# A gated-recurrence kernel with routed experts: chunk pieces in another order, and expert tiles from chunk 11 on

## The chip, the core and the metric

The kernel runs on one core of a Trainium2 chip. The metric is the time of one launch on the device, in microseconds (us). The engines are TensorE (PE: matmuls and transposes; its weight loads are PEld), VectorE (DVE), ScalarE (ACT), GpSimd (POOL) and SyncE (SP); each runs its own instructions in order and waits on semaphores. Sixteen DMA engines serve the loads and stores that SP, ACT and POOL issue.

## The reference

A gated linear recurrence over 4 batches, 8 heads, 768 steps and head dimension 48 gives rows of width 8 * 48 = 384. A router then picks two of eight experts for each of the 3072 rows, and the output is the weighted sum of the two experts' results.

```
for t in range(S):                                   # S = 768
    state = alpha[:, :, t, :, None] * state + k_t (outer) v_t
    y[:, :, t] = einsum('bhd,bhde->bhe', q[:, :, t], state)
x = y.transpose(0, 2, 1, 3).reshape(3072, 384)
noisy = x @ w_gate + log1p(exp(x @ w_noise)) * noise  # (3072, 8)
top2 = the two largest of each row; top2_w = softmax over them
for e in range(8):                                    # F = 1024
    for k in range(2):
        mask = top2[:, k] == e
        out[mask] += top2_w[mask, k, None] * (relu(x[mask] @ w1[e]) @ w2[e])
```

## The kernel before, in words

**Chunks.** The 3072 rows are 24 chunks of 128 steps (six to a batch). For chunk n, SP loads alpha, k, q and v. `prepare` (L252) turns alpha, k and q with TensorE transposes into a PSUM pool `tp` of two banks. ScalarE copies alpha into `a_all` (L257), runs a Relu over the same bank for a range test (L258), and copies k (L261). VectorE makes the running products `P_all` (scan, L264), q times them (L268), a reciprocal, and the reverse scan `over` (L273); GpSimd multiplies k by it (L275). `scores` (L281) has the k-q matmuls into two banks, the masked copies into `MT` (L291), and the transposes of k into `k_end` (L295, L297). `state` (L299) updates the state by a matmul (L309); `output` (L316) makes y (L189, L193) and copies it to `yT`; `turn_y` (L321) turns it and stores 128 rows of x (L203 to L206). `route` (L325) makes the logits (L211); after each third chunk it also runs `choose` (the two experts and their weights, VectorE and ScalarE, with table loads on ScalarE). `give` (L331) then ranks the rows (`rank`, L545; read by `picked`, L547), writes table entries by indirect DMA (L136), and plans tiles (`plan_tiles`: `total`, L579, and some 25 small VectorE operations up to L629). The PSUM pool `y` is a single bank: `s`, `lg`, `y`, `rank`, `total` and `count` share it.

**Tiles.** Three chunks are a unit, numbered from 0 to 7. After a unit is given, more full tiles of 128 rows of one expert are known. GIVEN says how many tiles stand ready after each unit: 0, 5, 11, 17, 23, 29, 35, and the rest; 51 tiles always run. Tiles 5 to 10, say, are those of unit 2, and unit 0 has none. A tile: its table rows (`load_tab`, L649), its w1 (1.5 MB, L657), a gather of its x rows (L675), a transpose `x_ps` and a VectorE copy `xt` (L684, L686), layer 1 in two halves (`h_ps`, L695, Relu L697), a gather of what the other expert has left of the rows (`prev` from `half_rows`, L714), layer 2 in two halves (`o_ps`, L707), the scaling (L724), a scatter into `half_rows` (L725), the sum (L731) and a scatter into the output (L732). `xt` has a single buffer, `prev` and w1 have two. All w2 (12.6 MB) is held on the chip, an expert's 1.5 MB per iteration over the first eight (L183).

**The order** is written by hand (L816 to L846): iteration n has a list of chunk pieces and a list of tile steps (four a tile), taken in turn, one of each. Tiles of unit u are beside iterations 3u+5 to 3u+7, two to an iteration at most, so the first is in iteration 8; unit 7's follow in one last iteration. In the iteration ahead of a unit's first tile, its tables and w1 are loaded, x is gathered, and, as the last piece, `turn_x` of that tile is run. The side buffer `half_rows` is zeroed at the start, by three DMAs of 1.5 MB from ScalarE's queue (L149 to L153).

Of the kernel before, what the change touches and what calls it, by code (L numbers as in the profile page):

```python
# [18 lines left out]
def kernel(  # L19
# [32 lines left out]
    C = 128  # L52
# [109 lines left out]
    def load_chunk(n, ins, vp):  # L162
        for x, src in (("a", alpha), ("k", k), ("q", q)):
            nc.sync.dma_start(out=ins[x][n % NIN][:, :, 0:D], in_=rows(src, n))
        vt = vp.tile([C, H, D], F32, name="vt")
        nc.sync.dma_start(out=vt, in_=rows(v, n))
        return vt
# [32 lines left out]
    def put_x(n, yT, on):  # L200
# [5 lines left out]
        nc.scalar.dma_start(out=x_rows[ds(n * C, C), :], in_=y_sb.rearrange("p j i d -> p (j i d)"))  # L206
# [8 lines left out]
    def fast_gla(on):  # L215
# [26 lines left out]
        def load(n):  # L242
            if n < NT:
                chunks[n] = {"v": load_chunk(n, ins, on["three"])}
# [7 lines left out]
        def prepare(n):  # L252
            if n >= NT:
# [4 lines left out]
            nc.scalar.activation(a_t, a_t, AF.Relu, bias=less_1, accum_out=above[:, n:n + 1])  # L258
            k_t = transposed(ins["k"][n % NIN])
            c["k"] = two.tile([C, NP, C], F32, name="k_P")  # L260
            nc.scalar.copy(c["k"], k_t)  # L261
            P_all = one.tile([C, NP * CB + 1], F32, name="P_all")
            P = P_all[:, 0:NP * CB].rearrange("p (j t) -> p j t", t=CB)
            nc.vector.tensor_tensor_scan(P_all[:, 0:NP * CB], a_all[:, 0:NP * CB],  # L264
                                         least.rearrange("p j t -> p (j t)"), 0.0, op0=ALU.mult, op1=ALU.max)
# [3 lines left out]


            over = one.tile([C, NP, CB], F32, name="over")
            nc.vector.reciprocal(out=P_all[:, CB::CB], in_=P_all[:, C::CB])
            nc.vector.tensor_tensor_scan(over.rearrange("p j t -> p (j t)")[:, :0:-1], a_all[:, :1:-1],  # L273
                                         P_all[:, :1:-1], 0.0, op0=ALU.mult, op1=ALU.max)
            nc.gpsimd.tensor_tensor(c["k"], c["k"], over[:, :, 1:CB], op=ALU.mult)  # L275
# [5 lines left out]
        def scores(n):  # L281
# [3 lines left out]
            sc = [on["sc"].tile([C, NP, C], F32, tag=f"sc{i}", name=f"sc{i}") for i in range(2)]  # L285
            for j in range(NP):
                for i in range(2):
                    r = ds(DP * i, D)
                    nc.tensor.matmul(sc[i][:, j, :], c["k"][r, j, :], c["q"][r, j, :], start=True, stop=True)  # L289
            for i in range(2):  # L290
                nc.vector.copy_predicated(MTs[n % 2][:, i], mask_upto, sc[i])  # L291
            if n % NCH != NCH - 1:
# [58 lines left out]
        return load, prepare, scores, state, output, turn_y, route, give, out_of_range  # L351


    def general_gla(es):
# [49 lines left out]
        def gla_prepare(n):  # L404
            vt = load_chunk(n, ins, vp)
# [226 lines left out]
    def experts(on):  # L632
# [80 lines left out]
        def get_half(i):  # L713
            get = nc.gpsimd.indirect_dma_start(out=prev[i % 2], out_offset=None, in_=half_rows,  # L714
                                               in_offset=bass.IndirectOffsetOnAxis(ap=wheres[i][:, 2:3], axis=0),
                                               bounds_check=N - 1, oob_is_err=False)
# [4 lines left out]
        def combine(i):  # L721
# [3 lines left out]
            put = nc.gpsimd.indirect_dma_start(out=half_rows,  # L725
# [15 lines left out]
    def tile_steps(i, do, units):  # L741
# [18 lines left out]
        def fourth():  # L760
            layer2(i, 1)
            combine(i)
# [137 lines left out]
```

## Time and profile before

| | us |
|---|---|
| median of 3 timed runs | 876.01 (875.53 to 878.22) |
| the profiled execution | 869.22 |
| its span, first to last instruction | 867.5 |
| TensorE busy in it | 773.0 |
| VectorE, ScalarE, GpSimd busy | 274.7, 198.4, 332.7 |
| mean granted TensorE clock | 0.951 of full |

A row of a timeline has start, duration, engine, line, operation, what is written and read, a count, and in brackets the engine's idle time ahead of it and what ended it. A row of the list of waits has the waiting and the awaited line, the us in total, how often, and the longest.

### The profile page before, as it was taken

The numbers are of one execution on the slowest core, as the hardware profiler recorded it, in microseconds if no ns is written. First come the engines' busy times: TensorE is split into PE (matmuls) and PEld (weight loads), VectorE is DVE, ScalarE is ACT, GpSimd is POOL, SyncE is SP. The second block draws the span as 40 slices with busy tenths as digits, with TensorE's granted clock in tenths as the row PEclk, the third lists the DMA queues.
The fourth block names the chain that finished last, engine by engine and source line by source line (L and its number), as shares of the span: only waits on it lengthen the run. The fifth ranks groups of instructions, "written<-read, shape, count | busy, mean of one in ns | idle before, by whom it ended". The sixth has DMA issues, their size and how long they took to land. (4 is left out here: it accounts for less than half of the span.)

```text
span 867.5 us, 14532 instructions
## 1 busy us (share of the span) xinstructions
PE 773.0 (89%) x5241; PEld 633.8 (73%) x5241; DVE 274.7 (32%) x969; ACT 198.4 (23%) x382; POOL 332.7 (38%) x436
## 2 busy tenths in 40 slices
PE   4878659997899999999998999999998999999992
PEld 3767548776687777877777877877876888888871
DVE  7455543234233531352324322431132111111110
ACT  2242402232123221321222222311121111111110
POOL 4224242326233732454334533353335333343331
PEclk9996859999799999999998999999999899999996
DMA  9997939443856277536673555426454345555530
GB/s 141 334 259 179 257 114 298 140 108 102 227 142 169 91 221 205 156 95 189 201 214 119 144 188 144 159 61 249 140 188 142 135 167 175 189 194 195 199 115 14
DMA packets 158532, 146.59 MB, mean 169 GB/s; under 512 B 119968, under 2 KB 132982, under 8 KB 158064
## 3 DMA queue, kind: packets, MB, share of 16 engines
q1 hardware_dynamic: 135904, 111.79, 44.6%
q0 software_dynamic: 14592, 23.75, 9.0%
q10 hardware_dynamic: 7952, 9.97, 3.5%
q8 instruction: 47, 0.77, 0.4%
q14 instruction: 37, 0.30, 0.1%
HBM read 131.95 MB, written 30.00 MB: 187 GB/s over the span
## 5 line engine op out<-in xcount | busy, mean ns | idle before, releaser
L695 PE MATMUL h_ps<-xt,w 128*128 128x128 f32 x2448 | 296.3, 281 | 8.6 <-DMA w<-in_moe_w_dram 4.7
L695 PEld LDWEIGHTS h_ps<-xt,w 128*128 128x128 f32 x2448 | 289.5, 197 | 17.1 <-DVE xt L686 5.7
L707 PE MATMUL o_ps<-w,h 128*128 x816 | 275.8, 487 | 0.0
L707 PEld LDWEIGHTS o_ps<-w,h 128*128 128x128 f32 x816 | 149.4, 190 | 89.3
L725 POOL DMA_INDIRECT half_rows<-o,where x51 | 58.4, 1146 | 264.7 <-ACT o L724 258.3
L697 ACT ACTIVATE h<-h_ps 128x512 f32<-128x512 f32 x102 | 60.8, 596 | 270.8 <-PE h_ps L695 270.8
L731 DVE TENSOR_TENSOR prev<-prev,o 128x384 f32<-128x384 f32 x51 | 28.5, 559 | 285.6 <-ACT o L724 153.0
L724 ACT ACTIVATE o<-o_ps,tab 128x384 f32<-128x384 f32 x51 | 29.7, 582 | 209.1 <-PE o_ps L707 207.0
L275 POOL TENSOR_TENSOR k_P<-k_P,over 128x512 f32<-128x512 f32 x24 | 28.4, 1183 | 111.1 <-DVE over L273 111.1
L675 POOL DMA_INDIRECT x_in<-x_rows,where x51 | 53.3, 1044 | 44.6 <-issue 20.4
L686 DVE COPY xt<-x_ps 128x384 f32<-128x384 f32 x51 | 28.3, 555 | 123.9 <-PE x_ps L684 123.9
L732 POOL DMA_INDIRECT out_dram<-prev,where x51 | 51.2, 1004 | 29.0 <-DVE prev L731 11.0
L714 POOL DMA_INDIRECT prev<-half_rows,where x51 | 53.0, 1039 | 21.0 <-issue 17.7
L136 POOL DMA_INDIRECT table<-entry,place_u x48 | 50.0, 1042 | 14.5 <-issue 12.2
L264 DVE TENSOR_TENSOR_SCAN P_all<-a_all,least 128x516 f32<-128x516 f32 x24 | 29.6, 1233 | 70.1 <-ACT a_all L257 68.3
L291 DVE COPY_PREDICATED MT<-upto,sc 128x512 f32<-128x512 uint32 x48 | 31.9, 719 | 17.8 <-PE sc L289 17.8
L684 PE MATMUL x_ps<-ident,x_in 128*128 128x128 f32 x153 | 27.1, 288 | 9.8 <-DMA x_in<-x_rows,where 9.8
L249 PE MATMUL tp<-ident,q_in 128*128 128x128 f32 x96 | 18.4, 322 | 18.1 <-ACT tp L258 17.4
L289 PEld LDWEIGHTS sc<-q_P,k_P 48*128 48x128 f32 x384 | 26.6, 210 | 8.1 <-issue 7.6
L289 PE MATMUL sc<-q_P,k_P 48*128 48x128 f32 x384 | 31.6, 310 | 0.0
L189 PE MATMUL y<-q_P,S 128*128 128x128 f32 x192 | 28.6, 297 | 2.8 <-ACT lgs L212 2.8
L273 DVE TENSOR_TENSOR_SCAN over<-a_all,P_all 128x515 f32<-128x515 f32 x24 | 29.6, 1235 | 0.8
(142 smaller groups left out, 649.8 us busy)
## 6 DMA issues: line engine op xcount, KB each, us to landing
w<-in_moe_w_dram SPq DMA_DIRECT2D x59, 1536.0 KB
a_in<-in_alpha_dram SPq DMA_DIRECT2D x24, 192.0 KB
k_in<-in_k_dram SPq DMA_DIRECT2D x24, 192.0 KB
q_in<-in_q_dram SPq DMA_DIRECT2D x24, 192.0 KB
vt<-in_v_dram SPq DMA_DIRECT2D x24, 192.0 KB
half_rows<-zeros ACTq DMA_DIRECT2D x3, 1536.0 KB
x_rows<-y_sb ACTq DMA_DIRECT2D x24, 192.0 KB
tab<-table SPq DMA_DIRECT2D x51, 2.0 KB
```

The source lines that it names most:

```text
L136: put = nc.gpsimd.indirect_dma_start(out=table, out_offset=bass.IndirectOffsetOnAxis(ap=place, axis=0), in_=entry, in_offset=None, bounds_ ...
L264: nc.vector.tensor_tensor_scan(P_all[:, 0:NP * CB], a_all[:, 0:NP * CB], least.rearrange("p j t -> p (j t)"), 0.0, op0=ALU.mult, op1=ALU.max)
L289: nc.tensor.matmul(sc[i][:, j, :], c["k"][r, j, :], c["q"][r, j, :], start=True, stop=True)
L291: nc.vector.copy_predicated(MTs[n % 2][:, i], mask_upto, sc[i])
L675: nc.gpsimd.indirect_dma_start(out=x_in[i % NB], out_offset=None, in_=x_rows[0:units * UT, :], in_offset=bass.IndirectOffsetOnAxis(ap=wher ...
L695: nc.tensor.matmul(h_ps[:, fo, :], w1[:, a, ds((part * FO // 2 + fo) * C, C)], xt[:, a, :], start=a == 0, stop=a == KO - 1)
L697: nc.scalar.activation(os_[i]["h"][part], h_ps, AF.Relu)
L707: nc.tensor.matmul(o["ps"], o["h"][part][:, f, :], w2[:, ds(o["e"], 1), fo, :].rearrange("p o d -> p (o d)"), start=fo == 0, stop=fo == FO ...
L714: get = nc.gpsimd.indirect_dma_start(out=prev[i % 2], out_offset=None, in_=half_rows, in_offset=bass.IndirectOffsetOnAxis(ap=wheres[i][:, ...
L724: nc.scalar.activation(o, o_ps, AF.Copy, scale=tab[:, 1:2])
L725: put = nc.gpsimd.indirect_dma_start(out=half_rows, out_offset=bass.IndirectOffsetOnAxis(ap=where[:, 1:2], axis=0), in_=o, in_offset=None, ...
L732: put = nc.gpsimd.indirect_dma_start(out=out, out_offset=bass.IndirectOffsetOnAxis(ap=where[:, 2:3], axis=0), in_=prev[i % 2], in_offset=N ...
```

## The change

The pieces of a chunk are cut finer and stand in another order: `prepare` becomes `alphas`, `keys` and `queries`; `scores` becomes `scores`, `masked` and `turn_k`; `load_chunk` leaves v to `load_v`, which comes behind `output`. `state` comes first in the iteration. `give` runs for chunk n-2 instead of n-1. The list of pieces is spread evenly over the tile steps. Tiles of unit u are beside iterations 3u+8 to 3u+10 (LAG = 8), so the first is in iteration 11. w2 is loaded in quarters of an expert, three an iteration over eleven iterations. `half_rows` is no longer zeroed; each chunk's rows are stored into it as well as into x. The router's loads and the table's clearing move behind iterations 0 and 1. Gathers from and scatters into `half_rows` name only the rows of units up to the tile's own.

```diff
-    def clear_half(on):
-        zeros = on.tile([C, KO * F], F32, tag="w1", name="zeros")
-        nc.vector.memset(zeros, 0.0)
-        for part in half_rows.rearrange("(i p r) d -> i p (r d)", p=C, r=KO * F // DM):
-            nc.scalar.dma_start(out=part, in_=zeros)
...
+    W2_PARTS = 4
-    def load_w2(e):
-        nc.sync.dma_start(out=w2[:, e], in_=moe_w2[e].rearrange("(a p) d -> p a d", p=C))
+    def load_w2(part):
+        e, f = divmod(part, W2_PARTS)
+        fs = ds(f * FO // W2_PARTS, FO // W2_PARTS)
+        nc.sync.dma_start(out=w2[:, e, fs], in_=moe_w2[e].rearrange("(a p) d -> p a d", p=C)[:, fs, :])
...
-        nc.scalar.dma_start(out=x_rows[ds(n * C, C), :], in_=y_sb.rearrange("p j i d -> p (j i d)"))
+        for dst in (x_rows, half_rows):
+            nc.scalar.dma_start(out=dst[ds(n * C, C), :], in_=y_sb.rearrange("p j i d -> p (j i d)"))
...
+        def keys(n):
...
             k_t = transposed(ins["k"][n % NIN])
             c["k"] = two.tile([C, NP, C], F32, name="k_P")
             nc.scalar.copy(c["k"], k_t)
+            nc.gpsimd.tensor_tensor(c["k"], c["k"], c.pop("over")[:, :, 1:CB], op=ALU.mult)
+        def queries(n):
...
             q_t = transposed(ins["q"][n % NIN])
             c["q"] = on["three"].tile([C, NP, C], F32, name="q_P")
             nc.vector.tensor_mul(c["q"], q_t, P[:, :, 1:C + 1])
...
-            get = nc.gpsimd.indirect_dma_start(out=prev[i % 2], out_offset=None, in_=half_rows,
+            get = nc.gpsimd.indirect_dma_start(out=prev[i % 2], out_offset=None, in_=half_rows[0:units * UT, :],
...
+        LAG = 8
-            u, part = divmod(n - UC - 2, UC)
+            u, part = divmod(n - LAG, UC)
-            if n >= UC + 2 and u < NU - 1 and GIVEN[u] > starts[u]:
+            if 0 <= u < NU - 1 and GIVEN[u] > starts[u]:
...
-                chunk = [lambda: prepare(n + 2), lambda: state(n), lambda: turn_y(n - 1), lambda: scores(n + 1),
-                         lambda: route(n - 1), lambda: output(n), lambda: load(n + 3), lambda: give(n - 1)]
-                if n < E:
-                    chunk.append(lambda: load_w2(n))
+                chunk = [lambda: (load(n + 3), state(n)), lambda: alphas(n + 2), lambda: keys(n + 2),
+                         lambda: scores(n + 1), lambda: (queries(n + 2), masked(n + 1)), lambda: route(n - 1),
+                         lambda: turn_k(n + 1), lambda: (output(n), load_v(n + 3)), lambda: turn_y(n - 1),
+                         lambda: give(n - 2)]
+                if n == 0:
+                    chunk.append(load_router)
+                if n == 1:
+                    chunk.append(lambda: clear_table(on["two"]))
+                chunk.append(lambda: [load_w2(i) for i in range(3 * n, min(3 * n + 3, E * W2_PARTS))])
                 if n == NT + 1:
                     chunk.append(out_of_range)
...
-                    chunk.insert(4, lambda: (load_w1(lo), [gather_x(i, u + 1) for i in some[:2]]))
+                    chunk.insert(6, lambda: (load_w1(lo), [gather_x(i, u + 1) for i in some[:2]]))
                     chunk.append(lambda: turn_x(lo))
-                for j in range(max(len(work), len(chunk))):
-                    if j < len(work):
-                        work[j]()
-                    if j < len(chunk):
-                        chunk[j]()
+                done = 0
+                for j in range(len(work)):
+                    work[j]()
+                    upto_j = len(chunk) * (j + 1) // len(work)
+                    for piece in chunk[done:upto_j]:
+                        piece()
+                    done = upto_j
+                for piece in chunk[done:]:
+                    piece()
```

On TensorE, a chunk's transposes beside a tile before (`h_ps` is layer 1, `tp` the transposes, `s` the state matmul):

```order
L695 MATMUL h_ps<-xt,w_1368 128x128 x12
L249 MATMUL tp<-ident,a_in_149 128x128 x4
L249 MATMUL tp<-ident,k_in_151 128x128 x4
L249 MATMUL tp<-ident,q_in_153 128x128 x4
L695 MATMUL h_ps<-xt,w_1368 128x128 x12
```

The same engine and place now, in an iteration with one tile (`sc` are the scores):

```order
L720 MATMUL h_ps<-xt,w_1985 128x128 x12
L332 MATMUL s_2140<-vt,k_end 128x96 x4
L255 MATMUL tp<-ident,a_in_149 128x128 x4
L720 MATMUL h_ps<-xt,w_1985 128x128 x12
L255 MATMUL tp<-ident,k_in_151 128x128 x4
L306 MATMUL sc_2201<-q_P,k_P 128x128
L306 MATMUL sc_2202<-q_P,k_P 128x128
...
L255 MATMUL tp<-ident,q_in_153 128x128 x4
```

The three groups of transposes stood together; layer 1 and the scores now stand between them.

On VectorE, the copy `xt` of a unit's first tile before, at the end of iteration 13 (`prev` is the sum of the two halves, `other` the next gather's test):

```order
L291 COPY_PREDICATED MT_169<-upto,sc_2769 128x512
L291 COPY_PREDICATED MT_169<-upto,sc_2770 128x512
L731 TENSOR_TENSOR prev_180<-prev_180,o 128x384
L686 COPY xt<-x_ps 128x384
L666 SCALAR_TENSOR_TENSOR other,before_it<-expert_idv,tab,given 128x8
```

The same copy now, at the end of iteration 16 (the rows up to `given` are the end of the plan that `give` makes):

```order
L651 TENSOR_REDUCE first<-row 128x6
L652 TENSOR_SCALAR plan<-first 128x6
L653 TENSOR_SCALAR plan<-of 128x6
L654 TENSOR_SCALAR given<-given 128x54
L756 TENSOR_TENSOR prev_180<-prev_180,o 128x384
L711 COPY xt<-x_ps 128x384
L691 SCALAR_TENSOR_TENSOR other,before_it<-expert_idv,tab,given 128x8
```

The plan, which was one iteration ahead of the copy, now stands directly in front of it.

On SyncE, the loads of one iteration of the alone stage before (`w_110` is w2):

```order
L166 DMA vt<-in_v_dram 128x8x48
L183 DMA w_110<-in_moe_w_dram 128x8x384
L164 DMA a_in_149<-in_alpha_dram 128x8x48
L164 DMA k_in_151<-in_k_dram 128x8x48
L164 DMA q_in_153<-in_q_dram 128x8x48
```

And now:

```order
L162 DMA vt<-in_v_dram 128x8x48
L182 DMA w_110<-in_moe_w_dram 128x2x384 x3
L158 DMA a_in_148<-in_alpha_dram 128x8x48
L158 DMA k_in_150<-in_k_dram 128x8x48
L158 DMA q_in_152<-in_q_dram 128x8x48
```

The order of the loads is the same; three quarters of an expert's w2 stand where one whole stood.

## Rows read from the trace of the kernel before

**Rows 1.** The page: busy us by engine, and TensorE's clock in 40 slices.
```profile
PE 773.0 (89%) x5241; PEld 633.8 (73%) x5241; DVE 274.7 (32%) x969; ACT 198.4 (23%) x382; POOL 332.7 (38%) x436
...
PEclk9996859999799999999998999999999899999996
```
**Rows 2.** Windows of the alone stage: busy us by engine, clock, DMA share, GB/s.
```profile
core 0: us, PE busy (x) PEld busy (x) DVE busy (x) ACT busy (x) POOL busy (x), PEclk, DMA share, GB/s
...
31.00:62.00 31.00, 25.79 (x238) 22.50 (x237) 15.84 (x24) 12.42 (x27) 7.29 (x14) 1.00 1.01 270
62.00:82.00 20.00, 16.23 (x99) 14.26 (x98) 9.08 (x35) 5.68 (x12) 8.91 (x14) 0.58 0.72 159
```
**Rows 3.** Waits: who waited for whom, us in total, times, longest.
```profile
PE tp L249 <- ACT tp L258: 17.4, 19, 1.3
...
PE total L579 <- DVE picked L547: 9.4, 7, 3.6
```
**Rows 4.** Timeline of TensorE in the alone stage, and the first h.
```profile
24.43 1.11 PE L249 MATMUL tp<-ident,k_in 128*128 128x128 f32 x4 [8.01 <-ACT k_end L297]
...
31.22 1.92 PE L189 MATMUL y<-q_P,S 128*128 128x128 f32 x8
...
61.10 1.13 PE L189 MATMUL y<-q_P,S 128*128 128x128 f32 x8 [0.35 <-ACT lgs L212]
...
66.14 0.59 PE L545 MATMUL rank<-chosen,before 128*128 128x24 f32 x2 [2.91 <-DVE past L535]
...
77.25 2.05 PE L189 MATMUL y<-q_P,S 128*128 128x128 f32 x8 [0.35 <-ACT lgs L212]
...
130.24 4.42 PE L695 MATMUL h_ps<-xt,w 128*128 128x128 f32 x24 [4.71 <-DMA w<-in_moe_w_dram]
```
**Rows 5.** DMA queues from 31 to 62 us: packets, MB, share of 16 engines.
```profile
q1 hardware_dynamic: 13543, 6.67, 85.6%
q10 hardware_dynamic: 405, 1.63, 14.5%
```
**Rows 6.** Timeline of TensorE beside tiles, and of two tiles alone.
```profile
161.96 2.84 PE L695 MATMUL h_ps<-xt,w 128*128 128x128 f32 x24
...
166.70 0.66 PE L249 MATMUL tp<-ident,q_in 128*128 128x128 f32 x4 [1.03 <-ACT tp L258]
...
171.07 2.75 PE L707 MATMUL o_ps<-w,h 128*128 x8
...
192.15 0.30 PE L545 MATMUL rank<-chosen,before 128*128 128x24 f32 x2
...
829.22 5.52 PE L695 MATMUL h_ps<-xt,w 128*128 128x128 f32 x48
...
840.06 5.52 PE L695 MATMUL h_ps<-xt,w 128*128 128x128 f32 x48
```
**Rows 7.** Timeline of TensorE at starts of units and at two late waits.
```profile
219.41 0.90 PE L684 MATMUL x_ps<-ident,x_in 128*128 128x128 f32 x3 [6.30 <-DMA x_in<-x_rows,where]
...
315.54 2.94 PE L695 MATMUL h_ps<-xt,w 128*128 128x128 f32 x24 [0.65 <-DVE xt L686]
...
472.17 0.60 PE L579 MATMUL total<-seen,ones 128*128 128x8 f32 x2 [3.56 <-DVE picked L547]
472.62 5.47 PE L695 MATMUL h_ps<-xt,w 128*128 128x128 f32 x24
...
673.21 0.59 PE L346 MATMUL count<-out_of,ones 128*128 128x2 f32 x2 [4.25 <-DVE out_of L344]
```
**Rows 8.** Timelines of VectorE (a plan's ends, a gather's offsets) and SyncE's queue.
```profile
283.99 0.20 DVE L547 TENSOR_TENSOR picked<-picked,rank 128x48 f32<-128x48 f32 x1
...
289.35 0.18 DVE L629 TENSOR_SCALAR given<-given 128x54 f32<-128x54 f32 x1
...
118.78 3.40 SPq L649 DMA_DIRECT2D tab<-table  x4
...
121.87 0.16 DVE L673 SCALAR_TENSOR_TENSOR where<-skip,tab 128x3 uint32<-128x3 f32 x1
```

More of the change, by code (lines that the diff above doesn't have):

```diff
@@ L243, in load, with load_v @@
             if n < NT:
-                chunks[n] = {"v": load_chunk(n, ins, on["three"])}
+                chunks[n] = {}
+                load_chunk(n, ins)
+        def load_v(n):
+            if n < NT:
+                chunks[n]["v"] = load_values(n, on["three"])
         def transposed(src):
@@ L250, in transposed, with alphas @@
             return tp
-        def prepare(n):
+        def alphas(n):
             if n >= NT:
@@ L261, in prepare @@
             nc.scalar.copy(c["k"], k_t)
[L262 to L265, printed above, removed]
+            nc.gpsimd.tensor_tensor(c["k"], c["k"], c.pop("over")[:, :, 1:CB], op=ALU.mult)
+        def queries(n):
+            if n >= NT:
+                return
+            c = chunks[n]
+            P = c.pop("P")
             q_t = transposed(ins["q"][n % NIN])
@@ L284, in scores @@
             c = chunks[n]
-            sc = [on["sc"].tile([C, NP, C], F32, tag=f"sc{i}", name=f"sc{i}") for i in range(2)]
+            c["sc"] = [on["sc"].tile([C, NP, C], F32, tag=f"sc{i}", name=f"sc{i}") for i in range(2)]
             for j in range(NP):
@@ L288, in scores, with masked, turn_k @@
                     r = ds(DP * i, D)
[L289 to L292, printed above, removed]
+                    nc.tensor.matmul(c["sc"][i][:, j, :], c["k"][r, j, :], c["q"][r, j, :], start=True, stop=True)
+        def masked(n):
+            if n < NT:
+                for i, sc in enumerate(chunks[n].pop("sc")):
+                    nc.vector.copy_predicated(MTs[n % 2][:, i], mask_upto, sc)
+        def turn_k(n):
+            if n < NT and n % NCH != NCH - 1:
+                c = chunks[n]
                 tp = on["tp"].tile([C, NP, C], F32, tag="tp", name="tp")
@@ L349, in out_of_range @@
             nc.vector.tensor_copy(out=again_i, in_=again)
-        return load, prepare, scores, state, output, turn_y, route, give, out_of_range
+        return (load, load_v, alphas, keys, queries, scores, masked, turn_k, state, output, turn_y, route, give,
+                out_of_range)
     def general_gla(es):
@@ L719, in get_half, with combine @@
             from_half.append(get.ins)
-        def combine(i):
+        def combine(i, units):
             o_ps, tab, where = os_.pop(i)["ps"], tabs.pop(i), wheres.pop(i)
@@ L756, in third @@
                 turn_x(i + 1)
-            get_half(i)
+            get_half(i, units[0])
             layer2(i, 0)
@@ L761, in fourth @@
             layer2(i, 1)
-            combine(i)
+            combine(i, units[0])
         return [first, second, third, fourth]
@@ L775 @@
         on = pools(es, "")
-        load, prepare, scores, state, output, turn_y, route, give, out_of_range = fast_gla(on)
+        (load, load_v, alphas, keys, queries, scores, masked, turn_k, state, output, turn_y, route, give,
+         out_of_range) = fast_gla(on)
         do = experts(on)
```

46 lines of the change are left out of this document (28 added, 18 removed).

## The prediction

> **What bounds the kernel now.** First the busy times: TensorE works 773.0 of 867.5 us, every other engine under 40% [rows 1]. So the time is TensorE's work, its idle time, and the time it runs at 1.2 instead of 2.4 GHz; the row of clocks shows the low level in slices near the start and in few later ones [rows 1]. Then TensorE's own timeline, by stage. Ahead of the first expert tile (its h at 130.24) chunks run alone; from there on tiles and chunks alternate.
>
> In the alone stage two things set the pace. The sixteen DMA engines are full, a share of 1.01 from 31 to 62 us [rows 2], and there three chunks take 61.10 − 31.22 = 29.9 us, 10.0 each [rows 4]. And where TensorE paused, its clock fell: the chunk with the wait of 2.91 us for `past` (rank at 66.14) took 77.25 − 61.10 = 16.2 us [rows 4], at a mean clock of 0.58 [rows 2].
>
> Beside the tiles, the list of waits [rows 3]: q's transposes wait for the Relu that frees one of the two `tp` banks, 19 times, 17.4 us; 14 of these stand beside tiles, with 14.3 us (166.70 is one [rows 6]). `total` waits for `picked`, 9.4 us, 9.1 of it beside tiles. The rest are starts of units, where `x_in`, `xt` or `count` is late [rows 7].
>
> The sum is made against the profiled execution, 869.22 us with a span of 867.5. The median of the timed runs is 876.01, 6.8 us more; I carry that difference over unchanged.
>
> **Chunks 8 to 10 leave the tiles: −22.4 us there.** The iteration from 161.96 to 192.15 is 30.19 us for two tiles and a chunk. A tile by itself takes 840.06 − 829.22 = 10.84 [rows 6]. So a chunk costs 30.19 − 21.68 − 1.03 (its q wait) = 7.48, three of them 22.4.
>
> **The q waits: −14.3 us.** Alphas, keys and queries now stand apart, with the scores or a step of a tile between them, so the Relu is done before q's transposes want the bank. Late next is the bank that x's transposes share with a and k; between them stands a step of layer 2, 2.75 us [rows 6], and a wait of 1.03 shows how little was missing with k's transposes alone between. Bounds 0 to −14.3; I take the whole.
>
> **`give` an iteration later: −9.6 us at `total`, +9.9 us at the starts of units.** Of the five gives beside tiles, four now stand ahead of the last step of layer 2, not behind the last `combine`, so `picked` no longer queues behind `prev` on VectorE. `total` then waits only for rank's own reader, some 0.4 us four times and 0.6 once, 2.2 in all. Before it was 9.1, and after the longest wait, 3.56, layer 1 took 5.47 us [rows 7] where the same row of 161.96 has 2.84 [rows 6]: about 2.7 us of low clock, 11.8 in all.
>
> But `turn_x` of a unit's first tile now comes behind the plan of the unit after it. VectorE copies `xt` only when that plan is done, 283.99 to 289.53, 5.5 us [rows 8], and layer 1 waits for `xt`. Unit 2: by my estimate the plan starts 1.2 us after the last matmul of layer 2 (o and `prev` come first), `xt` ends 7.4 after it, TensorE has 2.2 of work: 5.2 idle. Units 3 to 5: layer 2's second half covers 2.7 of it; from rank to `xt` are 7.2 us, TensorE's work 4.1: 3.1 idle. Unit 6 has `count` there, behind the longer last plan and `prev`: 4.5, and 0.65 for `xt`. Unit 7: 0.65. After idle times of 3.56 and 4.25 the clock fell (472.17, 673.21 [rows 7]), 2.7 us by the sum above; I charge that to units 2 and 6 and half of it to units 3 to 5. Sum: 7.9 + 3 × 4.45 + 7.85 + 0.65 = 29.8. Before: 6.30 + 0.65 + 2.7 at unit 2, 0.65 at four units, 4.25 + 0.65 + 2.7 at unit 7 [rows 7] = 19.9. So +9.9; bounds −4 (chain hidden, clock kept) to +19 (5.2 idle and the clock lost at each).
>
> **The alone stage: tile 0 starts at 137, not 130.24: +6.8 us.** The start: ScalarE no longer issues the clearing ahead of `k_end`, so the 8.01 us ahead of the k transposes at 24.43 go [rows 4], and y(0) starts near 23, not 31.22. The router's loads, now behind y(0) on ScalarE, take about 2 of that back. The pace: the first queue, with the loads of chunks and of w2, took 85.6% of 31 us for 13543 packets and 6.67 MB [rows 5]. An old iteration has 4 × 1024 packets of a chunk and 1024 of w2, 5120, hence 10.0 us. A quarter of w2 less is 256 packets or 0.39 MB: 0.5 us by packets, 1.8 by bytes, I take 1.1. The second copy of y is 0.2 MB on the other queue, which took 14.5% for 1.63 MB: 0.5 us [rows 5]. That makes 9.4; TensorE's own waits behind `choose` and `rank`, in six of the ten iterations, I leave in as 0.6: 10.0 an iteration (9.4 to 10.6), the old pace.
>
> Then y(1) starts at 35, y(9) at 35 + 8 × 10.0 = 115. Two us of y and 9 of v, w2 and a, k, q later the `tab` loads are issued, at 126 to 127. From there it is 3.25 us until the second tab's `where` is done (118.78 to 122.03 [rows 8]), then the plan, 5.5, and `xt`, 0.6: layer 1 near 137; w1 lands in that time. Bounds: 123, if TensorE's own 8.3 us a chunk (25.79 of 31 us for three [rows 2]) were the pace, to 150, with two chunks at 16.2.
>
> More and smaller w2 loads I cost at nothing: seven issues at 0.85 us (four `tab` issues take 3.40 [rows 8]) are 6.0 us on SyncE under 10.0 of DMA; without that cover it is rival 4. The Trainium skill, "DMA: Bandwidth & Descriptors", section Bandwidth, speaks against them: batch DMAs to 1 MiB or more for 75% of the peak, where a quarter of w2 has 384 KB. The trace differs so far, since the engines were full with loads of 192 KB making four fifths of the packets; by the rule the sum would come out where rival 4 does.
>
> The tail behind the last tile is the same work: 0.
>
> **Sum:** −22.4 − 14.3 − 9.6 + 9.9 + 6.8 = −29.6 us, so 876.0 − 29.6 = **846.4 us**.
>
> **Rivals.**
> 1. *Slower: the low clock.* The alone stage has eleven iterations now, and runs as chunk 4 did, 16.2 us instead of 10.0. From five such iterations on (29.6 / 6.2) the kernel is slower; eight of them, the third to the tenth, cost 50: **896 us**. For it: both waits for `past` were followed by long stretches at 1.2 GHz [rows 1, 2]. Against it: with `give` an iteration later that wait goes, and from 31 to 62 us, with DMA as full, the clock stayed. 0.10.
> 2. *The low clock behind `choose` alone*, three times in the stage, as ScalarE's table loads hold `yT` back: 3 × 6.2 = 18.6, **865 us**. 0.14.
> 3. *The q wait returns elsewhere*, on one of the same two banks: 14.3 not had, **861 us**. Against: the steps of 2.75 us between. 0.12.
> 4. *SyncE's issues of w2 hold the loads behind them*: two more per iteration at 0.85, eleven times, 18.7, **865 us**. Against: the cover of 4 us. 0.06.
> 5. *Better:* the pace is half way to TensorE's 8.3, or the three short idle times keep the clock and the chain is half hidden: 7 to 8 us, **838 us**. 0.12.
>
> That the change does not do what it says has no room of its own: the order shows each piece where the words put it.
>
> **How the numbers follow.** The forecast has 0.43, the rivals 0.10, 0.14, 0.12, 0.06, 0.12; 0.03 is two middling misses at once that end near 876. The range, 835 to 868, takes in the forecast and rivals 2 to 5 and leaves out rival 1 and that 0.03, with some room for two rivals together. A measurement of this kernel tells 0.3%, 2.6 us, from no change: faster 0.87, same 0.03, slower 0.10.
>
> **What would show it.** Right: q's transposes with no idle time ahead; `total` with some 0.4; the first h of units 2 to 5 waiting 3 to 5 us for `xt` while VectorE is in the plan; tile 0's h near 137 and a DMA share near 1 until then. Wrong: the low level in the row of clocks over much of the first 130 us; tile 0 past 150 or before 123; a new wait of 1 us or more in every iteration beside tiles.

## The result, and the profile after

The changed kernel took 851.74 us (847.3 to 854.57), 0.973 of the kernel before (interval 0.967 to 0.979). On a second chip, where it ran beside three of the experiments, it took 852.49 us, 0.980 (0.975 to 0.985). So the change is worth 18 to 24 us; 846.4 was forecast, with a range of 835 to 868.

The page of the profiled execution of 847.3 us, its head, the busy times and TensorE's clock; these lines answer to [rows 1]:

```profile
span 845.6 us, 14559 instructions
PE 767.9 (91%) x5241; PEld 629.8 (74%) x5241; DVE 271.6 (32%) x968; ACT 198.0 (23%) x382; POOL 335.9 (40%) x436
PEclk9898987999899999999999999998999999999997
```

The next view gives two windows of each kernel, the one ahead of the first h and the one from there to the last matmul: length, busy time of each engine, clock, DMA share. First the kernel before, then the changed one:

```profile
core 0: us, PE busy (x) PEld busy (x) DVE busy (x) ACT busy (x) POOL busy (x), PEclk, DMA share, GB/s
0.00:130.20 130.20, 90.69 (x641) 77.10 (x641) 70.53 (x174) 39.26 (x81) 43.69 (x111) 0.83 0.90 214
130.20:850.70 720.50, 682.30 (x4600) 556.73 (x4600) 203.64 (x794) 158.54 (x300) 286.87 (x323) 0.98 0.53 164
```

```profile
0.00:141.20 141.20, 106.49 (x872) 90.94 (x872) 91.97 (x244) 51.57 (x109) 57.24 (x132) 0.88 0.98 210
141.20:830.50 689.30, 661.44 (x4370) 538.88 (x4370) 179.08 (x723) 145.81 (x272) 276.52 (x302) 0.98 0.54 169
```

The stage of the tiles became 31.2 us shorter, of which 20.9 are TensorE's busy time (three chunks less) and 10.3 its idle time (38.2 before, 27.9 now). The alone stage became 11.0 longer, the tail 1.7 shorter (16.8 before, 15.1 now). Together 21.9, the difference of the two profiled executions. Forecast were −36.4, +6.8 and 0. (A few executions of the experiments below were disturbed, among them the profiled ones of e_turn and u_clear, whose lengths are not compared; the ratios leave such executions out, the medians do not.)

Where TensorE still waits beside the tiles: rows of its timeline at the starts of units and behind them, to be held against [rows 7]. The bracket holds the idle time ahead and what ended it.

```profile
218.93 0.39 PE L604 MATMUL total<-seen,ones 128*128 128x8 f32 x2 [0.58 <-DVE picked L572]
224.72 3.57 PE L720 MATMUL h_ps<-xt,w 128*128 128x128 f32 x15 [5.03 <-DVE xt L711]
318.12 7.25 PE L720 MATMUL h_ps<-xt,w 128*128 128x128 f32 x48 [2.88 <-DVE xt L711]
327.40 2.81 PE L732 MATMUL o_ps<-w,h 128*128 x8 [1.05 <-issue]
411.73 2.94 PE L720 MATMUL h_ps<-xt,w 128*128 128x128 f32 x24 [2.88 <-DVE xt L711]
419.52 0.27 PE L720 MATMUL h_ps<-xt,w 128*128 128x128 f32 x1 [1.03 <-issue]
502.91 7.25 PE L720 MATMUL h_ps<-xt,w 128*128 128x128 f32 x48 [2.88 <-DVE xt L711]
512.89 2.65 PE L732 MATMUL o_ps<-w,h 128*128 x4 [2.40 <-ACT h L722]
577.09 0.39 PE L604 MATMUL total<-seen,ones 128*128 128x8 f32 x2 [0.30 <-DVE picked L572]
584.71 0.46 PE L369 MATMUL count<-out_of,ones 128*128 128x2 f32 x2 [4.55 <-DVE out_of L367]
586.56 1.65 PE L720 MATMUL h_ps<-xt,w 128*128 128x128 f32 x6 [0.65 <-DVE xt L711]
652.43 2.85 PE L732 MATMUL o_ps<-w,h 128*128 x8 [0.98 <-ACT h L722]
657.01 3.17 PE L720 MATMUL h_ps<-xt,w 128*128 128x128 f32 x26 [1.40 <-DVE xt L711]
```

The waits of 2.88 to 5.03 for xt and the one of 4.55 for `count` were forecast. The four ahead of o at 327.40, of h at 419.52, and of o at 512.89 and 652.43 were not. They stand a few us behind a start, where ScalarE answers layer 1 late. At 512.24 it turns both halves of h at once, although TensorE had finished the first about five us earlier by its record:

```profile
512.24 1.08 ACT L722 ACTIVATE h<-h_ps 128x512 f32<-128x512 f32 x2 [11.93 <-remote]
```

ScalarE itself lost no time there. An engine lets another one go on by updating a semaphore, and the trace keeps the time of each update: TensorE's two signals for the halves were due at 507.48 and 510.16 by the ends of its matmuls, and they stand at 512.22 and 512.45. So a "late answer" below is a late signal; what goes with it is told in the last section.

The alone stage, against [rows 4, 8]: y(0), y(1), y(5), y(6) and y(9) of TensorE's timeline, SyncE's tab loads and w1 at its end, then x's transposes and the first h.

```profile
20.56 1.06 PE L188 MATMUL y<-q_P,S 128*128 128x128 f32 x8
31.53 1.91 PE L188 MATMUL y<-q_P,S 128*128 128x128 f32 x8
...
69.29 1.10 PE L188 MATMUL y<-q_P,S 128*128 128x128 f32 x8
83.61 1.91 PE L188 MATMUL y<-q_P,S 128*128 128x128 f32 x8
...
116.12 1.10 PE L188 MATMUL y<-q_P,S 128*128 128x128 f32 x8
```

```profile
128.82 3.16 SPq L674 DMA_DIRECT2D tab<-table  x4
132.50 0.38 SPq L682 DMA_DIRECT2D w<-in_moe_w_dram  x1
```

```profile
137.80 0.90 PE L709 MATMUL x_ps<-ident,x_in 128*128 128x128 f32 x3 [4.79 <-DMA x_in<-x_rows,where]
141.19 0.55 PE L720 MATMUL h_ps<-xt,w 128*128 128x128 f32 x1 [2.49 <-DMA w<-in_moe_w_dram]
```

### The profile page after: what moved, and what is told of

Read it like the earlier page. It is cut to its first block, busy times and chain, and to the rows that moved or that the text cites. A ratio compares the mean times of both kernels' runs of the same rounds, so it can differ in the third digit from the quotient of the medians.

```text
span 845.6 us, 14559 instructions
## 1 busy us (share of the span) xinstructions
PE 767.9 (91%) x5241; PEld 629.8 (74%) x5241; DVE 271.6 (32%) x968; ACT 198.0 (23%) x382; POOL 335.9 (40%) x436
## 5 line engine op out<-in xcount | busy, mean ns | idle before, releaser
L720 PEld LDWEIGHTS h_ps<-xt,w 128*128 128x128 f32 x2448 | 291.8, 197 | 30.0 <-DVE xt L711 17.3
L732 PE MATMUL o_ps<-w,h 128*128 x816 | 280.0, 491 | 4.5 <-ACT h L722 3.4
L750 POOL DMA_INDIRECT half_rows<-o,where x51 | 60.7, 1191 | 258.5 <-ACT o L749 257.2
L739 POOL DMA_INDIRECT prev<-half_rows,where x51 | 53.1, 1040 | 32.2 <-issue 18.7
L757 POOL DMA_INDIRECT out_dram<-prev,where x51 | 50.9, 998 | 17.4 <-issue 15.3
L267 DVE TENSOR_TENSOR_SCAN P_all<-a_all,least 128x516 f32<-128x516 f32 x24 | 31.3, 1304 | 53.1 <-ACT a_all L263 46.0
L337 POOL TENSOR_TENSOR S<-S,end 128x384 f32<-128x384 f32 x20 | 16.6, 830 | 37.7 <-DVE S L335 37.5
L709 PE MATMUL x_ps<-ident,x_in 128*128 128x128 f32 x153 | 26.5, 282 | 4.8 <-DMA x_in<-x_rows,where 4.8
L332 PE MATMUL s<-vt,k_end 128*128 128x96 f32 x160 | 23.2, 292 | 8.0 <-ACT yT L195 5.9
L306 PE MATMUL sc<-q_P,k_P 48*128 48x128 f32 x384 | 29.8, 298 | 0.0
```

Source lines behind the costliest of these rows:

```text
L306: nc.tensor.matmul(c["sc"][i][:, j, :], c["k"][r, j, :], c["q"][r, j, :], start=True, stop=True)
L720: nc.tensor.matmul(h_ps[:, fo, :], w1[:, a, ds((part * FO // 2 + fo) * C, C)], xt[:, a, :], start=a == 0, stop=a == KO - 1)
L732: nc.tensor.matmul(o["ps"], o["h"][part][:, f, :], w2[:, ds(o["e"], 1), fo, :].rearrange("p o d -> p (o d)"), start=fo == 0, stop=fo == FO ...
L750: put = nc.gpsimd.indirect_dma_start(out=half_rows[0:units * UT, :], out_offset=bass.IndirectOffsetOnAxis(ap=where[:, 1:2], axis=0), in_=o ...
L757: put = nc.gpsimd.indirect_dma_start(out=out, out_offset=bass.IndirectOffsetOnAxis(ap=where[:, 2:3], axis=0), in_=prev[i % 2], in_offset=N ...
```

## The experiments

Each kernel was timed beside the kernel before on the same chip, and its ratio is to that. c_after, u_q, u_give and e_turn shared one chip, u_clear, b_lag8, e_puts and e_turn_puts a second one, the others ran elsewhere.

| run | what it is | median us | ratio (interval) |
|---|---|---|---|
| c_after | the changed kernel | 852.49 | 0.980 (0.975 to 0.985) |
| u_q | alphas, keys, queries together again | 869.87 | 0.996 (0.993 to 0.999) |
| u_give | give(n-1) again | 864.84 | 0.991 (0.988 to 0.994) |
| e_turn | turn_x ahead of the plan | 854.21 | 0.975 (0.969 to 0.981) |
| u_clear | clearing back | 855.34 | 0.977 (0.973 to 0.982) |
| b_lag8 | before, first tile beside chunk 11 | 883.90 | 1.013 (1.008 to 1.018) |
| e_puts | table puts spread over the steps of tiles | 860.45 | 0.985 (0.980 to 0.990) |
| e_turn_puts | turn_x ahead, puts spread | 855.70 | 0.979 (0.975 to 0.983) |
| f_w1first | e_turn_puts, and w1 ahead of tab | 817.92 | 0.940 (0.936 to 0.943) |
| f_lag7 | first tile beside chunk 10, puts spread, w1 ahead of tab | 837.53 | 0.960 (0.956 to 0.964) |
| u_w2 | w2 whole, eight iterations | 849.38 | 0.968 (0.963 to 0.973) |
| f_turn_w1 | turn_x ahead of the plan, w1 ahead of tab | 817.56 | 0.939 (0.936 to 0.942) |

### The parts of the change, one by one

**c_after: the changed kernel once more.**

> The changed kernel once more, as the measure for the three beside it. First measured at 0.973 of the kernel before (0.967 to 0.979), median 851.7 us. Both theories: the same within 0.5%. Its trace tells one more thing: in the first trace ScalarE answered layer 1 late by 2 to 4 us, a few us behind the starts of units (326.7, 418.8, 512.3, 651.8). If that belongs to the kernel, it stands at the same places again; if it was a disturbance of one execution, it is gone or elsewhere.

It gave 0.980. Three of the four late answers stand at the same places of the program (329.0, 420.3 and 514.1 us here), the fourth, of 651.8, does not. So they are no chance of one execution; that they belong to the kernel does not follow, as the last section shows.

**u_q: the pieces of a chunk.**

```diff
-                chunk = [lambda: (load(n + 3), state(n)), lambda: alphas(n + 2), lambda: keys(n + 2),
-                         lambda: scores(n + 1), lambda: (queries(n + 2), masked(n + 1)), lambda: route(n - 1),
+                chunk = [lambda: (load(n + 3), state(n)), lambda: (alphas(n + 2), keys(n + 2), queries(n + 2)), lambda: None,
+                         lambda: scores(n + 1), lambda: masked(n + 1), lambda: route(n - 1),
```

> The changed kernel with alphas, keys and queries run together again as one piece, as in the kernel before; nothing else. Theory (the prediction's term of 14.3 us): q's transposes wait for the Relu again, about 1.0 us at each of 14 chunks beside tiles, 12 to 15 us more than the changed kernel, near 865; the alone stage is set by DMA and does not change. Rival (the pieces bought little, since the bank is late elsewhere or the chunk takes as long): at most 4 us more.

Its ratio is 0.016 above that of the changed kernel, 14 us; by the medians 17.4. In its list of waits the row of [rows 3] is back, in the changed kernel it is not in the list. Its two windows stand below the row:

```profile
PE tp L255 <- ACT tp L264: 19.3, 21, 1.3
```

```profile
0.00:148.30 148.30, 113.87 (x872) 96.74 (x872) 91.41 (x241) 51.72 (x109) 57.09 (x132) 0.88 0.93 199
148.30:856.80 708.50, 670.72 (x4370) 542.83 (x4370) 179.64 (x728) 144.98 (x273) 273.94 (x303) 0.97 0.54 165
```

Of the 21 waits 11, with 10.6 us, stand behind the first h. Against c_after's windows (under u_give) the stage of tiles is 15.5 us longer, 8.5 of them idle and 7.0 busy, so the theory holds there. The alone stage is 6 us longer too, which the theory did not say; single traces of that stage, in kernels that hardly touch it, have the first h anywhere from 138.50 (e_puts) to 145.90 (f_turn_w1), so this is not settled.

**u_give: the plan an iteration earlier.**

```diff
-                         lambda: give(n - 2)]
+                         lambda: give(n - 1)]
```

> The changed kernel with give(n-1) in place of give(n-2); nothing else. Theory by the terms of the prediction: the waits for total return (9 us, and 2.7 of low clock behind the longest), the wait for past returns in the alone stage with a long low clock behind it (6 us); against that the starts of units no longer wait for a plan (13.7 us and some 5 of low clock): between -3 and +4 us against the changed kernel. Rival 1: the later give is the gain that it seems, +8 to +12 us. Rival 2: the late answers of ScalarE behind the starts come from the table puts that give leaves running on GpSimd there; with give an iteration earlier they go as well, 8 us less.

It is 0.011 above the changed kernel, 10 us; by the medians 12.4. That is rival 1, but for another reason than a shorter stage of tiles. The two windows, u_give and then the changed kernel in the same group:

```profile
0.00:156.00 156.00, 119.86 (x873) 102.44 (x874) 90.89 (x244) 51.87 (x109) 60.62 (x136) 0.80 0.88 190
156.00:848.00 692.00, 657.99 (x4370) 535.30 (x4369) 178.53 (x723) 146.21 (x272) 273.98 (x299) 0.98 0.53 169
```

```profile
0.00:142.00 142.00, 109.62 (x871) 93.66 (x871) 90.58 (x238) 51.83 (x109) 56.33 (x132) 0.87 0.97 208
142.00:835.00 693.00, 663.73 (x4369) 541.90 (x4370) 179.98 (x730) 145.98 (x272) 276.91 (x303) 0.97 0.54 169
```

Beside the tiles the two are equal, 692 and 693 us, with other waits: those for `total` come to 6.8 us, not 1.8, and those for xt to 12.7, not 17.3; the theory had the latter nearly gone. The whole difference lies ahead of the first h, 155.6 against 142.7: TensorE is busy 10 us longer there for the same instructions, at a mean clock of 0.80, not 0.87, and the DMA engines fall from a share of 0.97 to 0.88. I read from these shares that with the earlier plan TensorE sets the pace of the alone stage more often, and with the later one DMA does. The waits that cost the clock in u_give are not one but many (`rank` for `past` has 3.0 us of them), so the step is shown, not its finest cause.

**u_clear: the clearing back, one copy of y.**

```diff
-        for dst in (x_rows, half_rows):
+        for dst in (x_rows,):
...
+            clear_half(on["two"])
             scores(0)
...
```

The gathers from and scatters into `half_rows` name all rows again, too.

> The changed kernel with the clearing of half_rows back ahead of the first scores, and y written to x_rows alone, as in the kernel before. Theory (the prediction's step on the start): y(0) comes 8 us later, and the 4.7 MB of zeros are moved in the alone stage, where the DMA engines set the pace, in place of the 2.2 MB of the second copies there: tile 0 comes 8 to 12 us later, and so the end, near 862. Rival (it was hidden: the loads go on while the clearing waits, and the stage catches up): tile 0 and the end within 3 us of the changed kernel.

Its ratio is that of the changed kernel, 0.977 between 0.973 and 0.980: by the time the rival holds, and ending the clearing is worth no more than some 4 us. The one trace does not show the stage catching up: y(0) starts at 25.91, 5.4 us later than in the changed kernel, y(9) at 122.69, 6.6 later, and the first h stands at 148.28. Where the time comes back is open.

**b_lag8: chunks 8 to 10 out of the tiles, alone in the kernel before.**

```diff
-            u, part = divmod(n - UC - 2, UC)
+            u, part = divmod(n - 8, UC)
-            if n >= UC + 2 and u < NU - 1 and GIVEN[u] > starts[u]:
+            if n >= 8 and u < NU - 1 and GIVEN[u] > starts[u]:
```

> The kernel before with one part of the change alone: the first tile stands beside chunk 11, not chunk 8. Theory by the prediction's terms: three chunks leave the tiles, -22.4 us, and three more run alone at 8.3 to 10 us each, +25 to +30: 2 to 8 us more than the kernel before. So this part alone is no gain, and the alone stage of the changed kernel paid for it by the clearing that went and the smaller w2 loads. Rival (the move is where the gain lies): 8 to 20 us less than the kernel before.

By the ratio it is 11.5 us slower than the kernel before in its group (1.013), by the medians 7.5. Its windows:

```profile
0.00:167.00 167.00, 115.60 (x872) 98.78 (x873) 94.13 (x245) 52.31 (x109) 57.25 (x134) 0.84 0.83 195
167.00:865.00 698.00, 661.36 (x4370) 536.62 (x4370) 180.75 (x723) 145.96 (x273) 275.73 (x300) 0.98 0.53 163
```

The stage of the tiles lost 22.5 us (720.5 to 698.0), the forecast's 22.4. The alone stage gained 36.8, not the expected 25 to 30. The DMA share is 0.83 and TensorE has 51 us without work there: three chunks alone ran at 12.3 us each.

**u_w2: w2 in whole experts over eight iterations.**

```diff
-    W2_PARTS = 4
+    W2_PARTS = 1
...
-                chunk.append(lambda: [load_w2(i) for i in range(3 * n, min(3 * n + 3, E * W2_PARTS))])
+                chunk.append(lambda: [load_w2(i) for i in range(n, min(n + 1, E))])
```

> The changed kernel with w2 as in the kernel before: a whole expert in one load, one in each of the first eight iterations, not three quarters in each of eleven. Theory (the prediction's price of nothing for the smaller loads; the bytes are the same and the engines full): tile 0 and the time within 3 us of the changed kernel. Rival 1 (the spread makes the alone stage even, and is part of its gain): tile 0 4 to 8 us later, and the time with it. Rival 2 (24 issues less on SyncE, as the rule on large loads has it): 4 to 10 us less.

The first h stands at 140.33, where the changed kernel has 141.19 and 142.70. So tile 0 is not later, nor is the end, and rival 1 falls. The ratio, 0.968 (0.963 to 0.973), overlaps the changed kernel's first measurement and lies below its second, on another chip each time. Whether the quarters cost nothing or up to 1%, which would be rival 2, is not settled; they bring nothing.

### The starts of units

**e_turn: the transposes of a unit's first tile ahead of the next plan.**

```diff
-                    chunk.append(lambda: turn_x(lo))
+                    chunk[11] = lambda plan_it=chunk[11]: (turn_x(lo), plan_it())
+                    chunk.append(lambda: None)
```

> The changed kernel with one edit: turn_x of a unit's first tile stands directly ahead of the plan of the unit after it, no longer behind it. Theory (the chain plan, xt, layer 1 is what the starts of units wait for): the idle times ahead of h of 5.03 and three of 2.88 us fall to about 0.65 or less, 11 us, and with them the low clock that follows, some 1.8 us at two or three of them: 11 to 17 us less than the changed kernel, near 838. Rival (something else is nearly as late there, x_in, w1 or the table puts): the waits change their name, x_ps or h waits for a DMA, and the time stays within 4 us of the changed kernel.

The waits for xt are gone from the list of waits, and the time is the changed kernel's, 0.975 against 0.980: the rival's number. The idle time has other names now, above all `tp` behind late answers of ScalarE:

```profile
PE tp L255 <- ACT tp L264: 11.0, 5, 4.8
```

**e_puts: the six table puts spread.** The late answers stood inside or right behind strings of eight to ten indirect DMAs on GpSimd, so the string was the next suspect.

```diff
...
+                put = lambda c=c, k=k: put_entries(place_u[:, k, c:c + 1], entry.bitcast(U32)[:, c, k, :])
+                put() if later is None else later.append(put)
...
                 for j in range(len(work)):
                     work[j]()
+                    if later:
+                        later.pop(0)()
...
```

Here `later` holds the puts of the last give, each as a call.

> The changed kernel with one edit: the six table puts that a give leaves on GpSimd no longer run in one string; where tiles run, one stands behind each of the next six steps of tiles. In the traces so far ScalarE answers layer 1 late by 2 to 7 us only inside or right behind strings of eight to ten indirect DMAs issued back to back on GpSimd, and 0.0 to 0.1 late elsewhere. Theory (the string holds the answers up): the late answers at the starts of units 3 to 5 go, and the idle time of TensorE that follows them, 1.2 + 1.2 + 2.4 + 1.0 in the first trace, with some low clock behind: 6 to 10 us less than the changed kernel (852.5 beside it last time), near 844. Rival (they come from something else, as the low clock or late records): they stay, and the time is within 3 us of the changed kernel.

It was no faster, 0.985 (860.45 us); 0.980 to 0.990 touches the changed kernel's interval. Late answers of 2 to 4 us remain, and a new wait is in the list, h for w1:

```profile
PE h_ps L722 <- DMA w<-in_moe_w_dram: 10.1, 4, 4.5
```

**e_turn_puts: both.**

> Both edits in the changed kernel: turn_x ahead of the plan, and the table puts one behind each step of a tile. By itself the first took away the waits for xt (13.7 us) and gave the time back in late answers of 4 to 7 us at every start of a unit. Theory (the string of puts took that gain): here neither is left, 16 to 25 us less than the changed kernel, near 832. Rival (the time at a start is set by a third thing that comes last either way): within 5 us of the changed kernel.

The rival holds once more: 855.70 us. But this trace names the third thing. Waits of TensorE, then a table put on GpSimd, SyncE's queue and TensorE at the start of a unit:

```profile
PE h_ps L722 <- DMA w<-in_moe_w_dram: 20.5, 5, 5.7
```

```profile
321.85 0.97 POOL L136 DMA_INDIRECT table<-entry,place_u  x1 [0.30 <-issue]
325.59 0.70 SPq L676 DMA_DIRECT2D tab<-table  x1
326.40 0.63 SPq L684 DMA_DIRECT2D w<-in_moe_w_dram  x1
336.59 1.65 PE L722 MATMUL h_ps<-xt,w 128*128 128x128 f32 x6 [5.53 <-DMA w<-in_moe_w_dram]
```

The w1 of a unit's second tile stands in SyncE's queue behind a tab load, and that load must wait until the table puts issued ahead of it have landed; here the last is the one of 321.85, which landed at 324.96. So w1 is issued at 326.40 and lands 10 us later, 5.5 after TensorE wants it.

**f_w1first: w1 ahead of the tab load.**

```diff
-                steps[0] = lambda go=steps[0]: (load_tab(i + 4), go())
+                steps[0] = lambda go=steps[0]: (go(), load_tab(i + 4))
```

> The last kernel with both edits (turn_x ahead of the plan, the puts spread) and a third: in a tile's first step the load of w1 is issued ahead of the tab load, not behind it. There the waits for xt and the late answers at starts of units were gone, and in their place h of a unit's second tile waited for w1, five times with 20.5 us: SyncE held its load behind a tab load that waits for the puts (issued at 326.4 to 327.0, landed 336.5). Theory (w1 was the third thing, and the last): these waits go, 15 to 20 us less than 855.7, near 838, 0.957 of the kernel before. Rival (a fourth thing is late at the starts as well): within 5 us of 855.7.

817.92 us, 0.940: 38 us less than e_turn_puts. The two ran on different chips, and the kernel before took 6 us less on this one (870.24 against 876.38), so 32 to 34 us are nearer to what the line is worth; the theory said 15 to 20. On one chip the three edits together stand 0.028 below u_w2, the changed kernel but for its w2 loads: 25 us. Windows of the stage of tiles, e_turn_puts and f_w1first:

```profile
142.90:839.00 696.10, 663.98 (x4370) 542.56 (x4370) 184.57 (x746) 146.75 (x273) 282.47 (x307) 0.97 0.55 168
```

```profile
142.60:800.80 658.20, 651.16 (x4371) 532.02 (x4371) 187.08 (x753) 146.28 (x273) 284.86 (x308) 0.99 0.57 177
```

The idle time falls from 32.1 to 7.0 us, and TensorE is busy 12.8 us less for the same 4370 matmuls, since its clock falls less often: a mean of 0.99, not 0.97. The expectation counted the waits alone.

**f_turn_w1: is the spread of the puts needed?** The edits of e_turn and f_w1first in the changed kernel, the puts in one string.

> The changed kernel with two edits of few lines: turn_x ahead of the plan, and w1 issued ahead of the tab load in a tile's first step; the table puts stay in one string. With the puts spread as well it took 817.9 us (0.940 of the kernel before), 658 us of it behind the first h, 6.9 idle and 9.2 at the low clock. Theory (w1 behind the tab load was what kept the starts of units late, and the late answers stood where w1 would have been waited for): the same without the spread, 818 within 4 us, TensorE idle beside tiles 7 to 11 us. Rival (the string of puts does harm by itself): the late answers of 2 to 7 us stay at units 2 to 6 and cost 2 to 5 us each with the clock behind them, 828 to 845.

817.56 us, 0.939 (0.936 to 0.942): the theory. This is the fastest version, 53 us less than the kernel before and, by the ratios, 30 to 36 less than the changed one. Its stage of tiles, and w1's issue and ScalarE's answers at the start of a unit:

```profile
145.70:803.90 658.20, 651.34 (x4372) 532.82 (x4372) 184.64 (x754) 146.04 (x272) 281.64 (x309) 0.99 0.57 178
```

```profile
307.02 0.37 SPq L682 DMA_DIRECT2D w<-in_moe_w_dram  x1
313.29 5.52 PE L720 MATMUL h_ps<-xt,w 128*128 128x128 f32 x48
316.17 0.60 ACT L722 ACTIVATE h<-h_ps 128x512 f32<-128x512 f32 x1 [2.10 <-PE h_ps L720]
318.85 0.60 ACT L722 ACTIVATE h<-h_ps 128x512 f32<-128x512 f32 x1 [2.08 <-PE h_ps L720]
```

TensorE is idle for 6.9 us, 4.5 of them the wait for `count`. The string of ten indirect DMAs is there as before, from 311.58 to 325.33 at this unit, and no answer is late at it. So with w1 early the string costs nothing that can be measured; whether it has a part in the late answers this trace cannot say (last section). Moving w1 alone, with turn_x left last, was not run in this kernel.

**f_lag7: the first tile one chunk earlier.**

```diff
-        LAG = 8
+        LAG = 7
...
-                chunk.append(lambda: [load_w2(i) for i in range(3 * n, min(3 * n + 3, E * W2_PARTS))])
+                chunk.append(lambda: [load_w2(i) for i in range(4 * n, min(4 * n + 4, E * W2_PARTS))])
```

with the puts spread and w1 ahead of the tab load, as above; turn_x stays last.

> The changed kernel with the first tile beside chunk 10 (w2 at four quarters in each of eight iterations, so that it is there), the puts spread, and w1 issued ahead of the tab load; turn_x stays where it was, since no plan stands in the iteration ahead of a unit now. Theory: the starts of units are free of the plan (13.7 us of waits and some 5 of low clock less), and the chunk that goes back to the tiles costs 7.5 there and saves 11 to 12 alone, as the 36.8 us for three in the test on the kernel before: 20 us less than the changed kernel, near 832, 0.955 or less. Rival (in the alone stage the DMA engines set the time, and w2 in fewer iterations gives the saving back): tile 0 no more than 3 us earlier, the time near 842.

837.53 us, between the two numbers. The first h stands at 139.17, 2 to 3.5 us earlier than in the changed kernel's two traces and within what traces with all eleven chunks show (138.50 to 145.90), though one chunk less runs ahead of it. So the 11 to 12 us of the theory are not there, as the rival said; the DMA share is 1.00 until then, its reason, and TensorE's clock is low as well, 0.78. The stage of tiles is 683.4 us, 25 more than in f_turn_w1: one chunk (7.5), and waits for xt and `total` with some low clock.

## Why the prediction was right, point by point

**Chunks 8 to 10, −22.4.** Right: −22.5 in b_lag8, 20.9 of it busy time; that the waits in the rest come out so near is luck, since they are others there (7 for q, not 14, and new ones in their place). But the chunks were paid for in full. Alone in the old kernel the move costs 36.8 us ahead of the first h and makes it 11.5 us slower. The gain of the changed kernel came from its other parts, which brought the first h from 167 to 141; half of that is `give`, as u_give shows.

**The q waits, −14.3.** Right: none left beside tiles, and 14 to 17 us back when undone, 15.5 of them in the stage of tiles by the traces.

**`total`, −9.6.** Right: 0.58 and four of about 0.30, 1.8 us in place of 9.1; 2.2 was said.

**Starts of units, +9.9.** The waits were right nearly to the tenth: 5.03, three of 2.88, 4.55 and 0.65, 1.40 make 20.3 us; the forecast's own waits (5.2, three of 3.1, 4.5 and 0.65, 0.65) make 20.3. The low clock behind them was near as well: layer 1 took 2.6, 1.7, 0.1, 1.7 and 2.6 us longer than at the full clock at units 2 to 6, where 2.7, three of 1.35, and 2.7 were charged.

**What the stage of tiles lacked** is 5.2 us of the forecast 36.4, and it is idle time. The four waits behind late answers, 1.05 + 1.03 + 2.40 + 0.98 = 5.5 us, are of that size; the sum has no term for them, as the trace of before shows none. Whether they are the kernel's is open (last section). What the account of the starts did miss is SyncE's queue, which it follows no further than the plan and xt. The w1 of a unit's second tile was nearly as late as xt of the first: in u_w2, after 2.88 us for xt at 500.44, TensorE waits for w1 too.

```profile
513.66 2.58 PE L720 MATMUL h_ps<-xt,w 128*128 128x128 f32 x21 [0.49 <-DMA w<-in_moe_w_dram]
```

In the sum that hardly showed, since the two lie one behind the other. In the experiments it is the likely reason why e_turn gained nothing until w1 was moved.

**`give` later.** The sum said that it brings nothing beside tiles (−9.6 + 9.9), and u_give agrees, 692 against 693. Its worth, 13 us, lies in the alone stage, where TensorE keeps its clock. The forecast had that only inside its pace of 10.0 us for every iteration, and as one reason against rival 1; that reason was right.

**Tile 0 at 137.** It stood at 141.19, so +11.0 in place of +6.8. y(0) came at 20.56 (23 said) and y(1) at 31.53 (35), but y(1) to y(9) took 84.6 us, 10.57 each where 10.0 was said. Two of the eight took 14.3 (69.29 to 83.61) and 13.9 us (92.81 to 106.73), at a clock of 0.74 and 0.89 and with the DMA engines full (1.01 and 1.09). That may be a mild form of rival 2, or DMA; no run separates them, and the 0.6 us that the sum left for TensorE's own waits was half of what was needed. Then two things were late that the forecast had hidden: x_in (x's transposes waited 4.79 us for it) and w1, issued at 132.50 and awaited for another 2.49 us, where the prediction said that it lands in time. The plan and xt, on which the step rested, were done at 139.30 and set nothing.

**The start, −8.** y(0) came 10.7 us earlier, more than was said. Whether that reaches the end is open: u_clear shows no loss by its time when the clearing returns, but its trace has the whole alone stage later. In the sum the step did not show, since y(1) came 3.5 us early and the slower pace took 4.6 back by y(9).

**w2 in quarters, 0.** Within 3 us by the first h; by the ratios the quarters cost 0 to 1%. That is less than the 18.7 us of rival 4 (865), which falls. The Trainium skill, "DMA: Bandwidth & Descriptors", section Bandwidth, has DMAs of 1 MiB or more as the way to 75% of the peak. By that rule the smaller loads should have slowed the stage; the traces hardly show it, a share of 0.98 and 210 GB/s with quarters of 384 KB against 0.99 and 215 with 1.5 MB in u_w2.

**Rivals.** None came in full. The parts do not add up to one number: by the ratios +11.5, −14 and −10 give −12 where c_after has −18, by the medians +7.5, −17.4 and −12.4 give −22 where it has −22. Whether a part is missing is not settled, and b_lag8 was run in the kernel before, not in the changed one.

**The working.** Two slips change nothing that hangs on them. By bytes a quarter of w2 costs 0.39 / 6.67 of the 26.5 us that the queue was busy, 1.6 us, not 1.8. And a measurement tells less than the 0.3% that the prediction gives it: the intervals here reach 0.3 to 0.6% to either side.

## What to carry to other kernels

Work moved out of a crowded stage is a gain only if the stage that takes it in has room: look at its DMA share and its clock first, and price the move alone. Where a stage starts late, follow every queue that feeds its first two steps, because two chains of nearly the same length hide each other, and taking away one can change nothing. In an in-order queue, issue the load that is wanted first ahead of the one that must wait. And before a strange wait is put down to the kernel, see whether all traces that have it were taken in the same way.

## What the runs showed of the hardware

A wait cost more than its length. u_w2 and f_w1first ran on one chip, and the records of both are complete (below). The window of u_w2, to be held against that of f_w1first:

```profile
140.30:828.40 688.10, 663.48 (x4370) 542.74 (x4370) 179.52 (x729) 146.21 (x272) 276.91 (x304) 0.97 0.54 169
```

The idle time of TensorE fell from 24.6 to 7.0 us and its busy time by another 12.3 for the same matmuls, 0.7 us for each microsecond of waiting, through the granted clock (a mean of 0.97 and 0.99 over the stage). Between e_turn_puts and f_w1first it was half a microsecond, 12.8 for 25.1.

The late answers go with the trace and not with the kernel. Five traces hold 10022 to 10686 updates of semaphores: before, u_w2, f_w1first, f_turn_w1 and f_lag7. The other nine hold only 7326 to 8183, for nearly the same programs, so that about a quarter of the records is missing. In the five, the Relu of layer 1 never begins more than 2.7 us behind the recorded end of its matmuls, and 4 to 6 of its 102 times more than 1 us; in the nine the worst is 3.0 to 7.2 us, and 16 to 26 are over 1 us. b_lag8, the kernel before but for three chunks, has late answers, and the trace of before has none; u_w2, the changed kernel but for its w2 loads, has none. The nine traces are the first of the changed kernel and all those from the two shared chips. So either the recording held the signals up or something on those chips did; no run separates the two, and neither the string of indirect DMAs nor w1's place is shown to cause or to end them.

They cost little by themselves: the stage of tiles is 688.1 us in u_w2, and 689.3 and 693.0 in the changed kernel's two traces. But the changed kernel, e_turn and e_turn_puts were measured only with them, f_w1first and f_turn_w1 only without, so a few us of the steps between those stay in doubt.
